# An attention and FFN kernel: pooled sums of v and the mask on TensorE, g applied at w_out's rounding, and a new order of the steps

## The chip, the cores and the metric

The kernel runs on one core of one Trainium2 chip. The metric is the device time of one execution in microseconds (us). A core has five engines that run side by side, each through its own list of instructions in a fixed order: PE (TensorE, matrix products; PEld is its weight load), DVE (VectorE), ACT (ScalarE), POOL (GpSimd) and SP (SyncE), which issues the transfers (DMAs). SBUF is the on-chip memory, PSUM the memory into which PE writes.

## The reference

For each of 8 batches and 8 heads (576 positions, 64 channels) two attentions are added: one over q, k and v averaged over groups of 4 positions, its result repeated 4 times, and one over the band of positions nearer than 4. The sum, as 4608 rows of 512, goes through an FFN with a SoLU and a layer norm.

```python
q_d, k_d, v_d = (t.reshape(B, H, S // 4, 4, D).mean(axis=3) for t in (q, k, v))
out_up = np.repeat(sm_attn(q_d, k_d, v_d), 4, axis=2)
mask = np.abs(pos[:, None] - pos[None, :]) < 4
scores = np.where(mask, scale * (q @ k.T), -1e9)
attn_out = out_up + softmax(scores) @ v
h = x @ w_in                                  # x: 4608 x 512, w_in: 512 x 1024
solu = h * softmax(h)
ln = (solu - mean) / np.sqrt(var + 1e-6) * g_ln
out = ln @ w_out                              # w_out: 1024 x 512
```

The weights come in as float64; the kernel takes their two 32-bit words apart itself.

## The kernel before

**Start.** `Weights.piece` turns 16 pieces of the weights (512 KB each; 0 to 7 are w_in, 8 to 15 w_out) into two parts, `hi` (`wi_h`, `wo_h`) and `lo` (`wi_l`, `wo_l`), of 128x512. A piece takes one pass of ACT (`L323`), four of DVE (`L325`, `L329`, `L334`, `L338`), for w_out a pass of ACT that multiplies by g (`L358`), then ACT's rounding to `hi` (`L360`) and POOL's subtraction that leaves `lo` (`L362`). `keep_clock` is 24 times two products of zeros that nobody reads (`L947`, tile `warm`), placed among the steps of PE.

**Attention of a batch.** `EarlyBatch` (batches 0 and 1) turns q and k on PE (`qp`, `kp`, `L478`) and copies them on ACT (`L484`); later batches turn them on DVE (`L411`, `L415`). Sums over 4 positions (`L367`) give `qd` and `kd`. The pooled v, `vd`, comes from v loaded a second time (`vs`, `L275`) and added up on POOL in two steps (`L434`, `L437`). `Local` does the band: ten windows of 64 positions, two at a time (u = 0 to 4). PE makes the scores (`sc`, `L614`), DVE adds the mask (`L632`) and takes the maximum (`L637`), POOL subtracts it (`L639`), ACT takes the exponential (`L641`), DVE sums and inverts (`L644`, `L648`), POOL multiplies (`L650`), PE turns the result (`plt`, `L660`), ACT copies it (`plT`, `L663`), PE multiplies by the window's v (`vw`; `xp`, `L670`), and the result is added to x (`L496`, `L498`). `Pooled` does the same for the averages, a pair of heads at a time (`sd` `L696`, `mxd` `L703`, `pd` `L711` to `L720`, `pdt` `L731`, `pdT` `L738` to `L743`, `po` `L752`).

**FFN.** Tile i holds 128 of the 4608 rows. `xhl` splits x into `xh` and `xl` (`L919`, `L922`); `ffn_in` is 24 products of 128x512 into `h` (`L770`), a maximum on DVE (`nmx`, `L778`), the exponential on ACT (`L782`), and `e` on DVE (`L785`), which frees h's only buffer. u goes out to memory and back (`L813`, `L845`), DVE turns it in blocks (`L866`), ACT and POOL split it (`uh` `L872`, `ul` `L874`), and `ffn_out` is 24 products into `o` (`L888`).

**What sets the order.** All steps are numbered in a plan of 2099; `ORDER` is a table that lists every number once, and the instructions are recorded in that sequence. Each engine runs its own in that order. Semaphores are added where one engine needs another's result.

Of the kernel before, what the change touches and what calls it, by code (L numbers as in the profile page):

```python
# [129 lines left out]
def pooled_local_attention_then_solu_ffn(  # L130
# [10 lines left out]
    nc = tc.nc  # L141
# [27 lines left out]

    EARLY = 2  # L170
    MASKED = 0
    W_PSUM = False
    WARM = 24

    def rows(n):
# [866 lines left out]
```

## Time and profile before

| | before |
|---|---|
| time, median of 3 runs | 602.74 us (602.57 to 603.37) |
| the profiled execution's own time | 602.74 us |
| its span, first to last instruction | 601.0 us |
| PE busy | 574.8 us, 96% |
| DVE, POOL, ACT busy | 396.5, 375.6, 361.8 us |
| granted PE clock, mean | 0.989 |

The time of a run is 1.74 us longer than the span of the same execution. Busy time is the union of an engine's instructions; two that follow each other overlap by some hundredths of a us in the records, so a sum of mean durations is a few per cent over the busy time.

### The profile page before, as it was taken

The page shows a single profiled execution, that of the slowest core. Times are in us where ns is not written, and L with a number is a line of the kernel's source. Part 1 is how long each engine was busy: PE and PEld are TensorE (multiplying, and loading weights), DVE is VectorE, ACT ScalarE, POOL GpSimd, SP SyncE. Part 2 cuts the span into 40 slices and gives each one's busy share as a digit, 9 for nine tenths or more (in the row PEclk, how much of TensorE's full clock was granted, in tenths as well). Part 3 has the DMA queues.
Part 4 walks back from the last instruction along what each step waited for, and adds up shares of the span by engine and source line. Part 5 has one row for each costly group of instructions (what it writes and reads, how often), then busy time and mean ns, then how long its engine had stood idle before and what let it go on. Part 6 is the DMA issues. An engine that isn't in the chain of part 4 may idle for free.

```text
span 601.0 us, 15341 instructions
## 1 busy us (share of the span) xinstructions
PE 574.8 (96%) x5912; PEld 447.1 (74%) x5912; DVE 396.5 (66%) x692; ACT 361.8 (60%) x800; POOL 375.6 (62%) x553
## 2 busy tenths in 40 slices
PE   6889789899999999999999999999999999999996
PEld 3666557677777777787877777777777878788785
DVE  5989999869747677766856767737655533643541
ACT  3758866577745566566664854657465655553443
POOL 2576668867784778678574777656786767332221
PEclk8979999899999999999999999999999999999999
DMA  8999776687769767766878567847416623124230
GB/s 231 238 251 254 140 183 146 164 178 162 195 144 189 171 167 186 170 148 175 190 151 201 143 173 182 185 114 195 97 59 188 146 89 114 63 88 151 96 123 35
DMA packets 203913, 94.34 MB, mean 157 GB/s; under 512 B 162496, under 2 KB 192704, under 8 KB 203840
## 3 DMA queue, kind: packets, MB, share of 16 engines
q1 hardware_dynamic: 203840, 93.37, 63.3%
q8 instruction: 46, 0.75, 0.6%
q14 instruction: 27, 0.22, 0.1%
HBM read 65.54 MB, written 27.79 MB: 155 GB/s over the span
## 4 chain that ended last, share of the span: by engine, by line
PE 75%; POOL 6%; DVE 5%; ACT 4%; SPq 4%; DMA 3%; issue 3%; POOLq 0%; DVEq 0%
PE o L888 31%; PE h L770 27%; PE xp L670 3%; PE plt L660 3%; PE po L752 3%; PE sc L614 2%; DMA qm<-in_q_dram 2%; SPq L245 2%; PE pdt L731 2%; PE sd L696 2%; POOL pl L639 2%; DMA v<-u 1%; SPq L264 1%; POOL pd L720 1%; DVE w L334 1%
## 5 line engine op out<-in xcount | busy, mean ns | idle before, releaser
L888 PE MATMUL o<-wo_h,uh 128*128 128x512 f32 x288 | 117.9, 409 | 0.8 <-ACT uh L872 0.7
L770 PE MATMUL h<-wi_h,xh 128*128 128x512 f32 x288 | 116.3, 404 | 0.6 <-DVE e L785 0.6
L770 PE MATMUL h<-wi_h,xl 128*128 128x512 f32 x288 | 114.3, 397 | 1.3 <-POOL xl L922 1.3
L888 PE MATMUL o<-wo_l,uh 128*128 128x512 f32 x288 | 114.5, 398 | 0.0
L770 PE MATMUL h<-wi_l,xh 128*128 128x512 f32 x288 | 114.1, 396 | 0.0
L874 POOL TENSOR_TENSOR ul<-v,uh 128x512 fp32r<-128x512 f32 x58 | 74.4, 1288 | 19.7 <-ACT uh L872 7.7
L778 DVE TENSOR_REDUCE nmx<-h 128x1 f32<-128x1024 f32 x36 | 43.9, 1219 | 63.8 <-PE h L770 63.8
L888 PE MATMUL o<-wo_h,ul 128*128 128x512 f32 x288 | 79.1, 396 | 0.4 <-DVE ul L874 0.4
L782 ACT ACTIVATE e<-h,nmx 128x1024 f32<-128x1024 f32 x36 | 40.0, 1112 | 51.0 <-DVE nmx L778 51.0
L888 PEld LDWEIGHTS o<-wo_h,uh 128*128 128x128 f32 x288 | 54.6, 190 | 15.6 <-ACT uh L872 1.4
L770 PEld LDWEIGHTS h<-wi_h,xl 128*128 128x128 f32 x288 | 54.2, 188 | 15.2 <-POOL xl L922 2.1
L770 PEld LDWEIGHTS h<-wi_h,xh 128*128 128x128 f32 x288 | 54.2, 188 | 14.8 <-issue 1.0
L888 PEld LDWEIGHTS o<-wo_h,ul 128*128 128x128 f32 x288 | 54.2, 188 | 14.0 <-DVE ul L874 0.8
L770 PEld LDWEIGHTS h<-wi_l,xh 128*128 128x128 f32 x288 | 54.3, 189 | 12.2
L888 PEld LDWEIGHTS o<-wo_l,uh 128*128 128x128 f32 x288 | 54.5, 189 | 11.8
L922 POOL TENSOR_TENSOR xl<-x,xh 128x512 fp32r<-128x512 f32 (+1 forms) x40 | 47.1, 1183 | 18.6 <-ACT xh L919 17.4
L807 ACT ACTIVATE e<-e,nmu 128x1024 f32<-128x1024 f32 x35 | 40.1, 1146 | 28.2 <-POOL nmu L790 28.1
L785 DVE SCALAR_TENSOR_TENSOR e<-h,e 128x1024 f32<-128x1024 f32 x36 | 43.7, 1214 | 19.9 <-ACT e L782 19.9
L650 POOL TENSOR_TENSOR pl<-pl,rsl 128x512 f32<-128x512 f32 x40 | 42.1, 1055 | 20.7 <-DVE rsl L648 18.2
L866 DVE STREAM_TRANSPOSE v<-v 128x512 f32<-128x512 f32 x70 | 46.3, 688 | 12.5 <-DMA v<-u 12.5
L872 ACT ACTIVATE uh<-v 128x512 fp32r<-128x512 f32 x70 | 42.9, 623 | 14.9 <-DVE v L866 11.0
L639 POOL TENSOR_TENSOR pl<-pl,mxl 128x512 f32<-128x512 f32 x40 | 41.8, 1052 | 9.0 <-DVE mxl L637 4.6
(95 smaller groups left out, 1076.1 us busy)
## 6 DMA issues: line engine op xcount, KB each, us to landing
u<-e SPq DMA_DIRECT2D x35, 512.0 KB
v<-u SPq DMA_DIRECT2D x140, 128.0 KB
vw<-in_v_dram SPq DMA_DIRECT2D x160, 64.0 KB
vs<-in_v_dram SPq DMA_DIRECT2D x32, 288.0 KB
out_dram<-osb SPq DMA_DIRECT2D x36, 256.0 KB
qm<-in_q_dram SPq DMA_DIRECT2D x96, 72.0 KB
km<-in_k_dram SPq DMA_DIRECT2D x96, 72.0 KB
w<-in_moe_w_out_dram SPq DMA_DIRECT2D x8, 512.0 KB
```

What stands on the lines that cost most here:

```text
L639: nc.gpsimd.tensor_tensor(out=pl, in0=pl, in1=max_bc, op=ALU.subtract)
L650: nc.gpsimd.tensor_tensor(out=pl, in0=pl, in1=rs.unsqueeze(3).broadcast_to([P, NPR, 2, W]), op=ALU.mult)
L770: nc.tensor.matmul(hps[:, n, :], src[:, cc, :], wt[:, cc, n * 512:(n + 1) * 512], start=(cc == 0 and src is xh and wt is wi_h), stop=(cc = ...
L778: nc.vector.tensor_reduce(out=nmx, in_=hf, op=ALU.max, axis=AX.X, negate=True)
L782: nc.scalar.activation(e, hf, AF.Exp, bias=nmx, scale=1.0, accum_out=se)
L785: nc.vector.scalar_tensor_tensor(out=e, in0=hf, scalar=1.0, in1=e, op0=ALU.mult, op1=ALU.mult, accum_out=su)
L807: nc.scalar.activation(e, e, AF.Identity, bias=nmu, scale=1.0)
L866: nc.vector.transpose(vg, vg)
L872: nc.scalar.activation(uh, tp, AF.Copy)
L874: (nc.vector if v is None or i in LATE else nc.gpsimd).tensor_tensor(out=ul, in0=tp, in1=uh.bitcast(F32), op=ALU.subtract)
L888: nc.tensor.matmul(o, src[:, j, :], wt[:, 4 * g + j, :], start=(g == 0 and j == 0 and src is uh and wt is wo_h), stop=(g == 1 and j == 3 a ...
L922: nc.gpsimd.tensor_tensor(out=l, in0=src, in1=h.bitcast(F32), op=ALU.subtract)
```

## The change

1. **Pooled sums of batch 0 on PE** (`SUMS_ON_PE = 1`). `vd` of batch 0 is no longer added up on POOL from a second load of v. `pool_steps` multiplies the local part's tiles `vw` by band matrices of zeros and ones: 20 products, two chunks (`vp`) of five windows and two halves; ACT copies one half of a chunk, DVE adds the other. `make_bands` builds the bands once (a memset on POOL, three sums on DVE). Batch 0 so needs all five `vw` ahead of its pooled part, and its four loads of `vs` (288 KB each) are gone.
2. **Mask by PE in batches 0 and 1** (`MASKED = 2`). Two products of 128x256 in bf16 (`ident_b` by `mask_b`) put the mask into the scores' bank, and the scores are added to it. DVE takes the maximum from PSUM and subtracts it itself, so POOL's subtraction and one step of the plan go, ten times in all. `keep_clock` multiplies `ident_b` in place of zeros.
3. **g at the rounding** (`G_LATE`). For w_out, g is the scale of ACT's rounding pass, and DVE forms `lo` as w times g minus `hi` in one instruction (`scalar_tensor_tensor`); the pass of ACT over w and POOL's subtraction go, eight times.
4. **Other engines** (`OTHER`). 145 steps in a second table run on another engine than usual: among them, new on DVE, are 11 `e<-e,nmu`, 25 `ul`, 17 `xl`, 11 each of `pl` minus maximum and `pl` times `rsl`, 9 `pd`, 6 pairs of the pooled sums, 10 `plT` and 8 copies to x; the first DVE pass of 9 weight pieces (`L325`) goes to POOL.
5. **A new order**: `ORDER` is another table (2088 steps now).

```diff
 ORDER = """
-181 0 182 1 2 3 165 25 183 166 4 5 6 184 167 185 24 26 186 187 188 27 7 8 173 32 168 169 170
...
+159 11 16 3 2 160 161 162 9 56 19 24 167 168 169 170 26 171 172 173 25 163 27 33 32 164 174 165
...
+OTHER = """
+29 84 95 104 161 174 185 209 217 225 257 265 273 281 355 498 518 519 523 565 567 573 592 598
...
-    MASKED = 0
-    W_PSUM = False
+    MASKED = 2
     WARM = 24
+    SUMS_ON_PE = 1
+    G_LATE = True
...
+    if MASKED:
+        filler = ident_b
...
+    GR = SD // 2
+    BAND = {0: (0, 16), 1: (3, 15), 3: (1, 15)}
+    bands = {}
+
+    def make_bands():
+        t = moe.tile([P, DFF], F32, tag="e", name="bands")[:, 0:3 * 160]
+        t = t.rearrange("p (r x) -> p r x", r=3)
+        nc.gpsimd.memset(t, 0.0)
+        by_half = ident.rearrange("p (h k) -> p h k", h=2)
+        for n, (r, (off, m)) in enumerate(BAND.items()):
+            nc.vector.tensor_reduce(
+                out=t[:, n, GR:GR + m],
+                in_=by_half[:, :, off:off + FAC * m].rearrange("p h (j i) -> p j h i", i=FAC),
+                op=ALU.add, axis=AX.XY,
+            )
+            bands[r] = t[:, n]
...
+    other = {int(n) for n in OTHER.split()}
+    now = [None]
+
+    def engine(usual, instead):
+        return instead if now[0] in other else usual
...
-            nc.vector.tensor_scalar(
+            engine(nc.vector, nc.gpsimd).tensor_scalar(
                 out=t, in0=t, scalar1=F64_LO, scalar2=F64_HI, op0=ALU.max, op1=ALU.min
             )
...
-                nc.scalar.activation(t, t, AF.Copy, scale=self.g[:, fc:fc + 1])
+                g = self.g[:, fc:fc + 1]
                 hi, lo = wo_h[:, fc, :], wo_l[:, fc, :]
+                if G_LATE:
+                    nc.scalar.activation(hi, t, AF.Copy, scale=g)
+                    yield
+                    nc.vector.scalar_tensor_tensor(
+                        out=lo, in0=t, scalar=g, in1=hi.bitcast(F32), op0=ALU.mult, op1=ALU.subtract
+                    )
+                    yield
+                    return
...
+        def pool_steps(self):
+            firsts = [-(-s0 // FAC) for s0 in starts]
+            ends = firsts[1:] + [SD]
+            for c in range(2):
+                tp = two_banks(ps_h, "h", f"vp_{self.b}_{c}")[0:GR]
+                at = tp.rearrange("p h (r a d) -> p h r a d", r=NPR, a=2)
+                ws = range(5 * c, 5 * c + 5)
+                for w in ws:
+                    s0, g0, g1 = starts[w], firsts[w], ends[w]
+                    at0 = GR - (g0 - GR * c)
+                    K = FAC * g1 - s0
+                    for half in range(2):
+                        nc.tensor.matmul(
+                            at[:, half, :, half ^ (w % 2), :],
+                            bands[s0 % FAC][half * W:half * W + K, at0:at0 + GR],
+                            self.vw[w // 2][half * W:half * W + K, w % 2],
+                            start=w == ws[0], stop=w == ws[-1],
+                        )
+                yield
+                vd = self.vd[:, c].rearrange("p h d -> p (h d)")
+                nc.scalar.activation(vd, tp[:, 0], AF.Copy)
+                yield
+                nc.vector.tensor_tensor(out=vd, in0=vd, in1=tp[:, 1], op=ALU.add)
+                yield
...
     def attention(bt):
-        values(bt)
+        by_pe = bt.b < SUMS_ON_PE
+        late = bt.b == 0
...
+        if by_pe:
+            if not bt.b:
+                step(make_bands)
+            for u in range(5):
+                step(bt.load_v, u)
+            row(bt.pool_steps(), 6)
+        else:
+            values(bt)
...
     for n in ORDER.split():
-        fn, args = plan[int(n)]
+        now[0] = int(n)
+        fn, args = plan[now[0]]
         fn(*args)
```

In the rows below a name is a tile with its indices and a buffer's number. Three places show the new order. The first is DVE's list where the last two pieces of w_out, 14 and 15, are made ready. Before:

```order
L644 TENSOR_REDUCE sml_4_1493<-pl_106 128x8
L648 RECIPROCAL rsl_4_1495<-sml_4_1493 128x8
L325 TENSOR_SCALAR w_14_1480<-w_14_1480 128x512
L325 TENSOR_SCALAR w_15_1497<-w_15_1497 128x512
L329 TENSOR_SCALAR w_15_1497<-w_15_1497 128x512
L329 TENSOR_SCALAR w_14_1480<-w_14_1480 128x512
L334 SCALAR_TENSOR_TENSOR w_15_1497<-w_15_1220,w_15_1497 128x512
L334 SCALAR_TENSOR_TENSOR w_14_1480<-w_14_1064,w_14_1480 128x512
L338 SCALAR_TENSOR_TENSOR w_15_1497<-w_15_1220,w_15_1497 128x512
L338 SCALAR_TENSOR_TENSOR w_14_1480<-w_14_1064,w_14_1480 128x512
```

Here piece 14 leaves DVE with its last row, and ACT and POOL do the rest. The same place of DVE's list after:

```order
L374 TENSOR_SCALAR w_15_1628<-w_15_1628 128x512
L423 TENSOR_REDUCE kd_1638<-kT_1472 128x144
L379 SCALAR_TENSOR_TENSOR w_15_1628<-w_15_1232,w_15_1628 128x512
L379 SCALAR_TENSOR_TENSOR w_14_1563<-w_14_1437,w_14_1563 128x512
L383 SCALAR_TENSOR_TENSOR w_15_1628<-w_15_1232,w_15_1628 128x512
L907 RECIPROCAL r_1660<-se_1374 128x1
L467 STREAM_TRANSPOSE kT_1472<-km_998 128x576
L471 STREAM_TRANSPOSE qT_1695<-qm_997 128x576
L383 SCALAR_TENSOR_TENSOR w_14_1563<-w_14_1437,w_14_1563 128x512
L423 TENSOR_REDUCE kd_1638<-kT_1472 128x144
L408 SCALAR_TENSOR_TENSOR wo_l<-w_15_1628,g_sb,wo_h 128x512
L408 SCALAR_TENSOR_TENSOR wo_l<-w_14_1563,g_sb,wo_h 128x512
```

The first pass of each piece is gone from the list (it is POOL's), steps of batch 2 stand in between, and the subtraction that makes `wo_l` ends the sequence on DVE. The second place is PE's list early in batch 0, around the third pair of windows. Before:

```order
L614 MATMUL sc_1_416<-kT_158,qT_157 64x64 x16
L731 MATMUL pdt_0_444<-ident,pd_0_269 72x64 x12
L614 MATMUL sc_2_463<-kT_158,qT_157 64x64 x16
L614 MATMUL sc_3_501<-kT_158,qT_157 64x64 x16
L478 MATMUL qp_2_527<-ident,qm_458 64x96 x12
L752 MATMUL po_0_542<-pdT_0_457,vd_304 64x144 x4
```

After:

```order
L691 LDWEIGHTS ident_b
L691 MATMUL sc_2_464<-mask_b,ident_b 128x256
L698 MATMUL sc_2_464<-kT_166,qT_165 64x64 x16
L510 MATMUL vp_0_488<-vw_0_346,bands 72x4x64 x4
L510 MATMUL vp_0_488<-vw_1_267,bands 72x4x64 x4
L510 MATMUL vp_0_488<-vw_2_424,bands 72x4x64 x2
```

The mask's products stand ahead of the scores, and the first chunk of the pooled sums has moved onto PE behind them. The third place is POOL's list in batch 0. Before:

```order
L362 TENSOR_TENSOR wi_l<-w_4_250,wi_h 128x4x4x32
L434 TENSOR_TENSOR vs_1_0_413<-vs_1_0_413 72x4x128
L437 TENSOR_TENSOR vd_304<-vs_1_0_413 72x256
L639 TENSOR_TENSOR pl_105<-pl_105,mxl_0_411 128x4x128
L720 TENSOR_TENSOR pd_2_434<-pd_2_434,rsd_2_440 128x432
L639 TENSOR_TENSOR pl_106<-pl_106,mxl_1_442 128x4x128
L650 TENSOR_TENSOR pl_105<-pl_105,rsl_0_495 128x4x128
```

After:

```order
L416 TENSOR_TENSOR wi_l<-w_4_358,wi_h 128x4x4x32
L806 TENSOR_TENSOR pd_2_432<-pd_2_432,rsd_2_519 128x432
L736 TENSOR_TENSOR pl_107<-pl_107,rsl_0_603 128x4x128
L370 TENSOR_SCALAR w_7_563<-w_7_563 128x512
L736 TENSOR_TENSOR pl_108<-pl_108,rsl_1_685 128x4x128
```

The pooled sums and the subtractions of the maximum are gone from it, and a first pass over a weight piece stands there.

More of the change, by code (lines that the diff above doesn't have):

```diff
@@ L26 @@
 ORDER = """
[99 rows of a table removed]
[99 rows of a table added]
+"""
+OTHER = """
[8 rows of a table added]
 """
@@ L233, in small_bank @@
     def small_bank(b, n):
-        return (ps_o, "o") if b < 2 and n % 2 and not W_PSUM and not WARM else (ps_t, "t")
+        return (ps_o, "o") if b < 2 and n % 2 and not WARM else (ps_t, "t")
     def load_q_k(t, b, pr):
@@ L320, in f32 @@
             w = moe.tile([P, DO], F32, tag="osb", name=f"w32_{n}", bufs=2)
-            t = ps_o.tile([P, DO], F32, tag="o", name=f"wb_{n}") if W_PSUM else w
+            t = w
             ti = t.bitcast(I32)
@@ L495, in accumulate @@
         if first:
-            nc.scalar.activation(x, part, AF.Copy)
+            copy(engine(nc.scalar, nc.vector), x, part)
         else:
@@ L616, in by_tensor @@
                         bt.qT[rows(par), pr, s0:s0 + W], bt.kT[rows(par), pr, s0:s0 + W],
-                        start=not early, stop=True,
+                        start=not early, stop=not early or pr == NPR - 1,
                     )
@@ L638, in by_tensor @@
                 yield
-                nc.gpsimd.tensor_tensor(out=pl, in0=pl, in1=max_bc, op=ALU.subtract)
+                engine(nc.gpsimd, nc.vector).tensor_tensor(
+                    out=pl, in0=pl, in1=max_bc, op=ALU.subtract
+                )
                 yield
@@ L662, in by_tensor @@
             plT = wk.tile([P, NPR, 2, W], F32, tag="plT", name=f"plT_{b}_{u}")
-            nc.scalar.activation(plT, pt, AF.Copy)
+            copy(engine(nc.scalar, nc.vector), plT, pt)
             yield
@@ L737, in steps @@
             yield
-            nc.scalar.activation(pdT[:, :, :, 0, :], pt[:, 0], AF.Copy)
+            copy(engine(nc.scalar, nc.vector), pdT[:, :, :, 0, :], pt[:, 0])
             yield
-            if b < 2:
-                nc.scalar.activation(pdT[:, :, :, 1, :], pt[:, 1], AF.Copy)
-            else:
-                nc.vector.tensor_copy(out=pdT[:, :, :, 1, :], in_=pt[:, 1])
+            copy(
+                engine(nc.scalar, nc.vector) if b < 2 else engine(nc.vector, nc.scalar),
+                pdT[:, :, :, 1, :], pt[:, 1],
+            )
             yield
@@ L806, in ffn_in @@
         else:
-            nc.scalar.activation(e, e, AF.Identity, bias=nmu, scale=1.0)
+            if engine(nc.scalar, nc.vector) is nc.scalar:
+                nc.scalar.activation(e, e, AF.Identity, bias=nmu, scale=1.0)
+            else:
+                nc.vector.tensor_scalar(
+                    out=e, in0=e, scalar1=1.0, scalar2=nmu, op0=ALU.mult, op1=ALU.add
+                )
         s = small.tile([P, 1], F32, tag="s", name=f"s_{i}", bufs=6)
@@ L940, in pooled_local_attention_then_solu_ffn @@
     weights = Weights()
-    idle = []
     def keep_clock(n):
-        if not idle:
-            idle.append(ps_o.tile([P, 512], F32, tag="o", name="warm"))
+        o = ps_o.tile([P, 512], F32, tag="o", name=f"warm_{n}")
         for _ in range(2):
             nc.tensor.matmul(
-                idle[0].rearrange("p (a n) -> p a n", n=P), zeros,
-                zeros.unsqueeze(1).broadcast_to([P, 4, P]), start=True, stop=True,
+                o.rearrange("p (a n) -> p a n", n=P), filler,
+                filler.unsqueeze(1).broadcast_to([P, 4, P]), start=True, stop=True,
             )
@@ L981, in attention @@
     def attention(bt):
-        values(bt)
-        local = [Local(bt, u, bt.b > 0) for u in range(5)]
-        pooled = [Pooled(bt, pr, bt.b == 0) for pr in range(NPR)]
-        for it in pooled + local if bt.b == 0 else local + pooled:
-            if isinstance(it, Local):
+        by_pe = bt.b < SUMS_ON_PE
+        late = bt.b == 0
+        local = [Local(bt, u, not late) for u in range(5)]
+        pooled = [Pooled(bt, pr, late) for pr in range(NPR)]
+        if by_pe:
[4 more added lines that the diff above has]
+            row(bt.pool_steps(), 6)
+        else:
+            values(bt)
+        for it in pooled + local if late else local + pooled:
+            if isinstance(it, Local) and not by_pe:
                 step(bt.load_v, it.u)
```

37 lines of the change are left out of this document (24 added, 13 removed), and 203 rows, old and new, of tables (ORDER, OTHER).

## The prediction

> **What bounds the kernel now.** I read the page first (busy shares), then the sums by stage, then the order of time around the end of the start-up stage, then the groups by line.
>
> ```profile
> span 601.0 us, 15341 instructions
> PE 574.8 (96%) x5912; PEld 447.1 (74%) x5912; DVE 396.5 (66%) x692; ACT 361.8 (60%) x800; POOL 375.6 (62%) x553
> ```
>
> PE is busy for 96% of the span, so over the whole kernel only less work on PE, or fewer gaps in it, can shorten the time. Where the gaps are, the busy times by stretch say (stretch, its length, then PE, PEld, DVE, ACT, POOL, the granted PE clock, DMA share, GB/s):
>
> ```profile
> 0.00:15.00 15.00, 9.96 (x58) 4.92 (x60) 8.22 (x17) 4.95 (x7) 3.44 (x13) 0.89 0.89 231
> 15.00:63.00 48.00, 41.02 (x811) 31.52 (x805) 43.98 (x77) 36.25 (x99) 30.29 (x29) 0.93 1.00 239
> 63.00:106.20 43.20, 37.84 (x462) 28.57 (x462) 42.27 (x70) 30.34 (x64) 31.54 (x34) 1.00 0.74 162
> 106.20:118.00 11.80, 9.34 (x218) 7.47 (x218) 9.91 (x17) 7.38 (x14) 10.36 (x13) 0.86 0.61 160
> 118.00:188.20 70.20, 70.08 (x700) 54.77 (x701) 50.46 (x91) 44.20 (x99) 50.27 (x76) 1.00 0.77 173
> 188.20:400.00 211.80, 211.46 (x2208) 166.51 (x2209) 143.45 (x252) 130.66 (x299) 146.38 (x211) 1.00 0.73 171
> ```
>
> From 118 us on PE has no gap worth the name (0.12 us to 188.2, 0.34 to 400). Up to 118 us it idles 5.04 + 6.98 + 5.36 + 2.46 = 19.8 us, and what is saturated there is DVE: 43.98 of 48.0, then 42.27 of 43.2. So the start-up is DVE's, and its length decides when PE's unbroken work begins. How the stage ends:
>
> ```profile
> 105.00 1.28 DVE L338 SCALAR_TENSOR_TENSOR w<-w,w 128x512 int32<-128x512 int32 x2
> 105.72 0.72 ACT L358 ACTIVATE w<-w,g_sb 128x512 f32<-128x512 f32 x1 [2.09 <-DVE w L338]
> 109.30 0.88 PE L660 MATMUL plt<-ident,pl 128*128 128x128 f32 x4 [2.46 <-ACT plT L663]
> 111.17 0.80 PE L888 MATMUL o<-wo_h,uh 128*128 128x512 f32 x1
> 113.25 0.40 PE L888 MATMUL o<-wo_l,uh 128*128 128x512 f32 x1
> ```
>
> DVE gives the last pieces of w_out at 106.28 (start and length of the first row), ACT stands 2.09 us waiting for them and has four passes (L358 and L360 of two pieces) queued ahead of the copy that PE needs, PE waits 2.46 us, and at 111.17 the second half of the first output tile starts. It is the last piece of PE work with a wait of that size ahead of it.
>
> **The change, part by part.** The sum is made at one point of PE's work: the product of that second half that first needs `wo_l` of piece 14, its sixth (four for pieces 12 and 13 ahead of it, then `wo_h` of 14); the useful work of PE behind that point is the same before and after. Before, it started at 113.25 (last row). In the new order DVE makes `wo_l` itself, so the point follows from when DVE is through its list up to there. These are the groups that carry the sum (busy us, mean ns of one):
>
> ```profile
> L325 DVE TENSOR_SCALAR w<-w 128x512 f32<-128x512 f32 x16 | 12.9, 814 | 5.6 <-ACT w L323 5.6
> L329 DVE TENSOR_SCALAR w<-w 128x512 int32<-128x512 int32 x16 | 9.2, 587 | 0.2
> L338 DVE SCALAR_TENSOR_TENSOR w<-w,w 128x512 int32<-128x512 int32 x12 | 8.0, 683 | 0.1
> L874 DVE TENSOR_TENSOR ul<-v,uh 128x512 fp32r<-128x512 f32 x12 | 9.0, 765 | 7.6 <-ACT uh L872 5.5 <-issue 2.1
> L632 DVE TENSOR_TENSOR pl<-sc,mask 128x512 f32<-128x512 f32 x40 | 26.7, 675 | 12.8 <-PE sc L614 12.7
> L743 DVE COPY pdT<-pdt 72x288 f32<-72x288 f32 x24 | 10.6, 444 | 14.5 <-ACT pdT L738 14.5
> L411 DVE STREAM_TRANSPOSE kT<-km 128x576 f32<-128x576 f32 x24 | 18.1, 759 | 0.0
> L367 DVE TENSOR_REDUCE kd<-kT 128x144 f32<-128x576 f32 x32 | 23.4, 738 | 0.8 <-ACT kT L484 0.6
> L648 DVE RECIPROCAL rsl<-sml 128x8 f32<-128x8 f32 x40 | 8.1, 203 | 1.9
> ```
>
> *DVE, added up to `wo_l` of 14.* Eight `wo_l`: the nearest row is `ul` (same output, two inputs in SBUF), 8 x 0.765 = 6.1. Four `pdT`, 1.8. One kT copy and the two additions to `vd` from PSUM, as L632, 2.0. One `wi_l`, 0.8. The bands: no row shows them; between L648 and L367, 3 x 0.2 to 0.7; they read few elements, so 0.25 each, 0.8; two casts at 0.2, 0.4. Work of batch 2 that now stands ahead (two transposes, one `kd`, one reciprocal), 2.4. Sum 14.3.
>
> *DVE, taken away.* Nine first passes over weight pieces, 9 x 0.814 = 7.3. The mask changes nothing here: L632 and the maximum become a maximum and a subtraction, two passes over 512 each.
>
> Net 7.0; in the records neighbours overlap (two of 0.683 took 1.28 above), so some 6.4. Before, DVE had 8.22 + 43.98 + 42.27 = 94.5 us of work to 106.2; after, 100.9.
>
> *POOL.* It loses, in the start-up, work of these rows, and gets nine passes that no row shows on POOL (between 0.7, as the smaller L437, and 1.4, as L362; I take 1.05, as L639):
>
> ```profile
> L362 POOL TENSOR_TENSOR wi_l<-w,wi_h 128x512 fp32r<-128x512 f32 x8 | 11.0, 1375 | 24.1 <-ACT wi_h L360 24.1
> L362 POOL TENSOR_TENSOR wo_l<-w,wo_h 128x512 fp32r<-128x512 f32 x8 | 10.4, 1299 | 11.2 <-ACT wo_h L360 11.1
> L434 POOL TENSOR_TENSOR vs<-vs 72x512 f32<-72x512 f32 x32 | 41.4, 1293 | 0.6
> L437 POOL TENSOR_TENSOR vd<-vs 72x256 f32<-72x256 f32 x32 | 23.8, 742 | 2.5
> L639 POOL TENSOR_TENSOR pl<-pl,mxl 128x512 f32<-128x512 f32 x40 | 41.8, 1052 | 9.0 <-DVE mxl L637 4.6
> ```
>
> Lost: 10 x 1.05 + 4 x (1.29 + 0.74) + 1.4 + 8 x 1.30 = 30.4; got: 9.5; so 21 of the 30.29 + 31.54 + 3.4 us it had to 106.2. POOL is no bound there; but its work delays DVE's:
>
> ```profile
> 11.09 1.37 POOL L362 TENSOR_TENSOR wi_l<-w,wi_h 128x512 fp32r<-128x512 f32 x1 [8.57 <-ACT wi_h L360]
> 11.37 1.64 DVE L338 SCALAR_TENSOR_TENSOR w<-stage,w 128x512 int32<-128x512 int32 x1
> 21.71 0.41 DVE L325 TENSOR_SCALAR w<-w 128x512 f32<-128x512 f32 x1
> 537.18 1.29 POOL L922 TENSOR_TENSOR xl<-x,xh 128x512 fp32r<-128x512 f32 x1
> 537.99 1.63 DVE L874 TENSOR_TENSOR ul<-v,uh 128x512 fp32r<-128x512 f32 x2 [0.23 <-ACT uh L872]
> ```
>
> Alone a pass of L325 takes 0.41 us (third row), on the mean 0.814. L338 at 11.37 ends at 13.01, 0.55 after POOL's end, 0.96 over the mean of 0.683. The `ul` pair of 537.99 ends at 539.62, 1.15 after POOL's end, and two free ones take 1.28 as the L338 pair does: they ran when POOL was through, some 0.3 over. So of the passes that stay, 7 x 0.40 (L325), 16 x 0.18 (L329 against 0.41) and that 0.96 are waits: 6.6. With a third less work on POOL (21 of 65) a third of it goes, 2.2 us; the ends are nothing and all 6.6. That gives 100.9 - 2.2 = 98.7 us.
>
> The Trainium skill (SBUF — State Buffer, "Who interferes with whom") states this as a rule: a DVE instruction with two SBUF inputs, and GpSimd instructions that read SBUF, shut each other out for a whole instruction. The trace agrees (the 537.99 row). By the rule, what moves from POOL to DVE keeps the wait and only changes the engine that pays for it; what it would do to the time is the second rival.
>
> *DVE's idle time.* Before: 6.78 us in the first 15 us, 4.02 to 63, 0.93 to 106.2. The first stays: it is the arrival of the first pieces. Of the second a known piece is this:
>
> ```profile
> 38.43 0.61 DVE L703 TENSOR_REDUCE mxd<-sd 128x3 f32<-128x432 f32 x1 [1.54 <-PE sd L696]
> ```
>
> That `sd` stood on PE behind `po`, whose `vd` came from POOL, the queue that loses the sums and subtractions. I take 1.0 of the 4.02 as gained; the ends are 4.02 gained and 3 us lost, the latter if the hops over POOL that the nine passes add (ACT, POOL, DVE) stand in the way. So 10.7 us idle, and DVE is through at 98.7 + 10.7 = 109.4. The point that was at 113.25 comes 3.8 us earlier.
>
> *PE, added.* Twenty products for the mask and twenty for the sums.
>
> ```profile
> 57.81 0.60 PE L947 MATMUL warm<-zeros 128*128 128x512 bf16 x2
> 51.85 0.71 PE L752 MATMUL po<-pdT,vd 72*64 72x144 f32 x8
> ```
>
> A mask product has half the columns of a warm one: 20 x 0.15 = 3.0. Four products of `po` (eight records) take 0.71; at 256 columns in place of 144 that is 0.32 each, 6.3 for twenty, 3.2 if halves run side by side and 12.6 if they stand apart as `po`'s do not. In all 6 to 16, I take 9. All stand in the stretch where PE idles 19.8 us and does 24 x 0.60 = 14 us of `warm` (24 pairs, the first row's length for each), which stay, some at other places. DVE sets the pace there, so 9 us cost nothing as long as PE's own work to the point, which then leaves some 11 us of idle, is not the longer one. At 16 us it leaves 4, and part of it would show.
>
> *ACT* loses eight passes of L358 and gets two copies of `vp`; *SP* loses four `vs` loads (1.2 MB) and brings five `vw` forward; the DMA share is 1.00 to 63 us, but DVE's waits there are on PE and ACT, so this is worth nothing to the sum.
>
> *Behind the point.* Up to the ninth tile's maximum (188.2 before) DVE had 9.91 + 50.46 = 60.4 us of work; by the build it now has some 15 two-input steps of POOL more there, and copies, 74 in all, in 79 us. PE then waits where a DVE step comes late; the first places are the scores of batch 2 and the second output tile. I take 1.6 of the 3.8 us as given back. From 188.2 DVE's load goes from 68% (143.45 of 211.8) to some 80%, which I cost at nothing: a step that is late by a POOL instruction has other tiles' products of PE in between.
>
> **Sum.** 601.0 - 3.8 + 1.6 = 598.8 us span; the execution shown was itself the median run, 1.74 us above its span: 600.5 us.
>
> **The rivals.**
>
> *No difference.* DVE is through at 100.9 + 11.7 = 112.6 (no relief, idle as before): the gain at the point is 0.6 us, and as much of new waits takes it. For it: DVE's list is longer, not shorter. Time 602.7.
>
> *Slower: the port.* In the 79 us behind the point DVE is full. Each of its 15 new two-input steps can find POOL at work: 0.3 us in the 537.99 pair, and up to the 1.29 of POOL's `xl` if that has just begun. At 0.5 us each it is 7.5 us, DVE then needs 81 of 79, and batch 2's scores and tiles 4 to 8 come late on PE. If the point also comes at 112.6 and half of the 7.5 reaches PE: 602.7 - 0.6 + 3.8 = 606. It decides once the new waits pass the slack of about 5 us. Against it: DVE kept 98% busy from 63 to 106 with the same neighbour.
>
> *Much faster.* All idle of 15 to 63 us but 1 us goes (3.0), and most of POOL's delays (another 2.5): 600.5 - 2.0 - 2.5 = 596. For it: POOL loses a third of its work, ACT eight passes of L358 (8 x 0.72 = 6 us).
>
> **How the numbers follow.** Forecast (598 to 601.5) 0.37, much faster 0.15, no difference 0.20, slower 0.28. What a measurement here can tell from no change is 0.2%, 601.5 to 604. The range goes from 594.5, below the much faster case, to 608, above the slower one. Faster 0.52, same 0.20, slower 0.28.
>
> **What would show it.** Right: the last `wo_l` on DVE near 109, DVE over 95% busy from 15 to 185 us, PE without gaps from some 115, `vp` and the mask's products with PE idle around them. Wrong: PE gaps between 115 and 190 that end on DVE; `ul`, `xl` or `pl` on DVE with means above 0.9 us; PE idle to 118 below 8 us, so that PE's added work shows; or a first weight piece that is ready later.

## The result: 1.0% slower, and the profile after

| | before | after |
|---|---|---|
| time, median (range, runs) | 603.06 us (602.57 to 604.32, 4) | 608.89 us (608.08 to 610.96, 4) |
| ratio to before, 95% interval | | 1.0099 (1.0074 to 1.0124) |
| profiled execution: time, span | 602.74, 601.0 us | 608.08, 605.9 us |

Executions of one kernel differ by up to 1.7%, and a trace shows one of them.

The page of the changed kernel, its head (busy time, share of the span, instructions):

```profile
span 605.9 us, 15391 instructions
PE 580.7 (96%) x5972; PEld 446.9 (74%) x5972; DVE 478.9 (79%) x814; ACT 337.4 (56%) x764; POOL 290.1 (48%) x450
```

PE has 5.9 us more of busy time, POOL 85 us less, DVE 82 us more. The busy times by stretch, for the same stretches as in the prediction (PE, PEld, DVE, ACT, POOL, granted PE clock, DMA share, GB/s):

```profile
0.00:15.00 15.00, 11.10 (x112) 5.70 (x112) 9.42 (x23) 4.63 (x7) 5.23 (x13) 1.00 0.88 260
15.00:63.00 48.00, 42.26 (x769) 30.39 (x766) 42.64 (x77) 33.52 (x94) 25.46 (x20) 1.00 0.87 219
63.00:106.20 43.20, 37.84 (x490) 27.20 (x489) 42.23 (x71) 28.82 (x61) 26.96 (x25) 0.96 0.71 160
106.20:118.00 11.80, 10.55 (x165) 7.84 (x167) 11.80 (x19) 5.44 (x9) 6.01 (x12) 1.00 0.54 140
118.00:188.20 70.20, 69.36 (x778) 54.64 (x774) 66.06 (x113) 41.31 (x94) 42.73 (x65) 1.00 0.80 179
188.20:400.00 211.80, 208.69 (x2182) 162.74 (x2181) 176.41 (x298) 121.28 (x284) 108.41 (x171) 1.00 0.66 159
```

Up to 118 us PE idles 3.90 + 5.74 + 5.36 + 1.25 = 16.3 us (19.8 before), so most of its new work went into idle time; DVE has no idle left between 106.2 and 118 us. From 118 to 400 us PE idles 0.84 + 3.11 us where it idled 0.12 + 0.34. The granted clock of PE is not what made the kernel slower: behind 118 us it is 1.00 in both, and ahead of it 1.00, 1.00, 0.96 and 1.00 in these stretches, where before it was 0.89, 0.93, 1.00 and 0.86. The end of the start-up, on DVE and on PE (timeline: start, length):

```profile
110.96 1.43 DVE L383 SCALAR_TENSOR_TENSOR w<-w,w 128x512 int32<-128x512 int32 x1
112.31 0.74 DVE L423 TENSOR_REDUCE kd<-kT 128x144 f32<-128x576 f32 x1
112.97 1.40 DVE L408 SCALAR_TENSOR_TENSOR wo_l<-w,g_sb,wo_h 128x512 fp32r<-128x512 f32 x2
113.19 0.49 PE L980 MATMUL o<-wo_h,uh 128*128 128x512 f32 x1 [0.52 <-ACT wo_h L406]
114.42 0.50 PE L980 MATMUL o<-wo_l,uh 128*128 128x512 f32 x1 [0.74 <-DVE wo_l L408]
```

The last two `wo_l` end at 114.37, and the product that the prediction counted to (the first with `wo_l` of piece 14) starts at 114.42, released by them. Before, it started at 113.25. PE's instructions ahead of it and behind it are the same in number in both traces, but for the 60 records of the new products, all ahead. So the 4.9 us of span split exactly: 1.2 us ahead of the point, and 605.9 - 114.4 = 491.5 in place of 601.0 - 113.25 = 487.75 behind it, 3.7 us. Forecast were -3.8 and +1.6. Of the 3.7 us behind the point, 2.5 are idle time of PE (8.9 in place of 6.4); the other 1.2 are longer busy time of the same products, for which no run gives a cause. What PE waited for behind the point, up to 560 us (us in total, times, longest; the five largest of changed, then the two of before):

```profile
PE h L856 <- DVE e L871: 1.2, 2, 0.8
PE o L980 <- ACT osb L987: 0.9, 2, 0.7
PE o L980 <- ACT uh L963: 0.8, 1, 0.8
PE po L838 <- DVE x L582: 0.4, 1, 0.4
PE xp L756 <- DVE pdT L269: 0.3, 1, 0.3
PE sc L614 <- issue: 0.9, 1, 0.9
PE pdt L731 <- ACT pd L711: 0.3, 1, 0.3
```

### The profile page after: what moved, and what is told of

The parts are those of the page before. It is cut to its first block, busy times and chain, and to the rows that moved or that the text cites. A ratio compares the mean times of both kernels' runs of the same rounds, so it can differ in the third digit from the quotient of the medians.

```text
span 605.9 us, 15391 instructions
## 1 busy us (share of the span) xinstructions
PE 580.7 (96%) x5972; PEld 446.9 (74%) x5972; DVE 478.9 (79%) x814; ACT 337.4 (56%) x764; POOL 290.1 (48%) x450
## 4 chain that ended last, share of the span: by engine, by line
PE 65%; DVE 14%; DMA 8%; SPq 4%; issue 4%; ACT 3%; POOL 1%; DVEq 0%; POOLq 0%; ACTq 0%
PE o L980 27%; PE h L856 24%; PE xp L756 3%; PE sc L698 2%; PE plt L746 2%; PE po L838 2%; DMA w<-in_moe_w_in_dram 2%; PE sd L782 2%; PE pdt L817 1%; SPq L309 1%; SPq L290 1%; DMA vs<-in_v_dram 1%; DVE sml L730 1%; DMA u<-e 1%; DVE nmx L864 1%
## 5 line engine op out<-in xcount | busy, mean ns | idle before, releaser
L966 POOL TENSOR_TENSOR ul<-v,uh 128x512 fp32r<-128x512 f32 x33 | 43.4, 1317 | 52.1 <-ACT uh L963 40.4
L856 PEld LDWEIGHTS h<-wi_l,xh 128*128 128x128 f32 x288 | 54.3, 189 | 11.9
L987 ACT ACTIVATE osb<-o,s 128x512 f32<-128x512 f32 x36 | 24.5, 682 | 40.5 <-PE o L980 12.2
L736 POOL TENSOR_TENSOR pl<-pl,rsl 128x512 f32<-128x512 f32 x29 | 31.2, 1079 | 27.9 <-DVE rsl L734 27.9
L1014 POOL TENSOR_TENSOR xl<-x,xh 128x512 fp32r<-128x512 f32 x23 | 30.2, 1315 | 25.7 <-ACT xh L1011 25.4
L966 DVE TENSOR_TENSOR ul<-v,uh 128x512 fp32r<-128x512 f32 x37 | 29.0, 794 | 12.0 <-ACT uh L963 11.9
```

The source lines that it names most:

```text
L736: engine(nc.gpsimd, nc.vector).tensor_tensor(out=pl, in0=pl, in1=rs.unsqueeze(3).broadcast_to([P, NPR, 2, W]), op=ALU.mult)
L856: nc.tensor.matmul(hps[:, n, :], src[:, cc, :], wt[:, cc, n * 512:(n + 1) * 512], start=(cc == 0 and src is xh and wt is wi_h), stop=(cc = ...
L966: (usual if v is None else engine(usual, nc.vector)).tensor_tensor(out=ul, in0=tp, in1=uh.bitcast(F32), op=ALU.subtract)
L987: nc.scalar.activation(osb, o, AF.Copy, scale=s)
L1014: engine(nc.gpsimd, nc.vector).tensor_tensor(out=l, in0=src, in1=h.bitcast(F32), op=ALU.subtract)
```

## The experiments

All were timed in five rounds against the kernel before (whose median was 602.2 to 603.0 us in these groups). For each, the point is where the first product with `wo_l` of 14 starts in its trace, and the rest is the span of that execution less the point. Both belong to the one execution whose time the third column gives.

| kernel | time, us | traced, us | ratio to before (95%) | point | rest |
|---|---|---|---|---|---|
| before | 603.06 | 602.74 |  | 113.25 | 487.75 |
| changed | 608.89 | 608.08 | 1.0099 (1.0074 to 1.0124) | 114.42 | 491.5 |
| e1 passes back on DVE | 608.06 | 607.37 | 1.0078 (1.0053 to 1.0103) | 113.64 | 491.7 |
| e2 moves behind undone | 626.20 | 625.15 | 1.0374 (1.0343 to 1.0406) | 113.87 | 509.5 |
| e3 no moves | 626.07 | 622.77 | 1.0372 (1.0340 to 1.0405) | 111.62 | 509.4 |
| e4 products twice | 612.81 | 612.84 | 1.0157 (1.0125 to 1.0190) | 118.49 | 492.1 |
| e5 products left out | 607.98 | 611.32 | 1.0083 (1.0052 to 1.0114) | 116.17 | 492.9 |
| e6 g late for two pieces | 614.85 | 614.88 | 1.0192 (1.0167 to 1.0217) | 121.36 | 491.7 |
| e7 sums back on POOL | 611.68 | 607.96 | 1.0161 (1.0123 to 1.0199) | 114.27 | 491.9 |
| e9 one pass left out | 603.95 | 601.45 | 1.0022 (1.0000 to 1.0044) | 108.59 | 490.6 |
| h1 new start, old tail | 609.96 | 611.27 | 1.0118 (1.0090 to 1.0147) | 115.47 | 493.9 |
| h2 old start, new tail | 611.61 | 613.97 | 1.0148 (1.0118 to 1.0177) | 114.79 | 497.4 |
| b1 before, g late | 608.62 | 610.02 | 1.0104 (1.0073 to 1.0134) | 120.63 | 487.6 |
| b2 before, g late for two | 605.23 | 603.51 | 1.0042 (1.0019 to 1.0064) | 113.45 | 488.3 |
| b3 before, masked | 598.18 | 598.35 | 0.9924 (0.9894 to 0.9954) | 109.86 | 486.7 |
| b4 before, sums | 609.51 | 610.10 | 1.0103 (1.0066 to 1.0140) | 120.96 | 487.3 |
| b6 before, masked, g late | 605.22 | 607.22 | 1.0051 (1.0024 to 1.0078) | 117.80 | 487.2 |
| b12 masked, POOL kept early | 617.85 | 621.34 | 1.0263 (1.0220 to 1.0306) | 132.18 | 487.4 |
| b13 masked, POOL kept in place | 604.74 | 606.38 | 1.0038 (1.0010 to 1.0066) | 117.04 | 487.6 |
| b15 before, masked, sums | 607.57 | 604.44 | 1.0081 (1.0050 to 1.0112) | 116.28 | 485.9 |

The last column is the first finding. Leave the two joined kernels (h) and the two without moves (e2, e3) aside: every kernel with the tail of before has a rest of 485.9 to 488.3, every one with the changed tail 490.6 to 492.9, though their points differ by up to 22 and 13 us. So the 3.7 us behind the point go with the tail. In all of these the tail follows a variant of its own start-up; what h1 and h2, which cross the two, add to that stands below.

One part of the change is not named among its five and has no run of its own: each pair of products of `keep_clock` now writes a tile of its own, where before all 24 wrote the same one. The kernels e and h1 do it the new way, b and h2 the old one. In the traces of before and changed only the first of these products waits, for its input (to 2.3 and 3.3 us).

### What sets the changed start-up

e1: the nine first passes go back to DVE.

```diff
-29 84 95 104 161 174 185 209 217 225 257 265 273 281 355 ...
+29 84 95 104 174 355 ...
```

> The changed kernel with one thing undone: the nine first passes over weight pieces (L370) go from POOL back to DVE. Theory A (the end of DVE's list sets the start-up, and POOL's passes of 1.97 us hold DVE's next passes up: L374 at 0.711, L379 at 0.876, L383 at 0.796 us where free ones take 0.43 and 0.69, together 8 us): DVE gets 9 x 0.41 to 0.81 = 3.7 to 7.3 us of work and loses most of the 8 us of waits and the hops over POOL; time 605 to 607. Theory B (PE's added products, some 7 us, set the time): no change, 608.4 to 609.4. Theory C (the steps moved to DVE behind the start-up make PE wait): no change either.

608.06 us, as much as the changed kernel within the intervals, and not the 605 to 607 of theory A; the point 0.8 us earlier. Nine passes more on DVE cost nothing, or: taking them off had gained nothing. Up to the point DVE is busy 104.3 us and idle 9.3, in place of 102.5 and 11.9.

e4 and e5: the new products issued twice, and for the most part left out.

```diff
-                for a in range(2):
+                for a, last in ((0, True), (1, True), (0, False), (1, False)):      # e4; the sums: for _ in range(2)
-                ws = range(5 * c, 5 * c + 5)
+                ws = range(5 * c, 5 * c + 2)                                        # e5; the mask's products are gone
```

> The changed kernel with each of the 40 new products on PE (20 for the mask, 20 for the sums) issued twice, same result. They are 10.4 us of busy time in the records, some 7 us in which PE takes nothing else. Theory A (DVE sets the start-up, PE has 16 us of idle there): at most 1.5 us more, 608.5 to 610.5. Theory B (PE's added work sets the time): 615 to 617.

> The changed kernel without the 20 mask products and without 12 of the 20 products of the sums (the softmax of two batches is then not masked and the pooled sums take two of five windows); everything else, the order and DVE's steps, as changed. Issued twice, the 40 products cost 3.9 us in the first group of runs. Theory A (DVE's list sets the start-up; the second copy only overfilled PE): 608 to 609, less than 1 us gained. Theory B (PE's products stand in the chain of the start-up: DVE waits for scores and sums that come behind them): 604 to 606.

Twice: 3.9 us more, between the two theories. Left out: 0.9 us less, inside the intervals (the traced execution took 611.32 us, so its late point says nothing). The products once are covered by PE's idle time; a second copy no longer is (in that trace DVE is busy 38.3 of the 48 us from 15 to 63 us, in place of 42.6: it then waits for PE).

e9: DVE's last pass over the eight pieces of w_out is left out.

```diff
-            nc.vector.scalar_tensor_tensor(out=w.bitcast(I32), in0=lo, scalar=29, in1=ti, ...
+            if n < 8:
+                nc.vector.scalar_tensor_tensor(out=w.bitcast(I32), in0=lo, scalar=29, in1=ti, ...
```

> The changed kernel without DVE's last pass (L383) over the eight pieces of w_out, so that the lowest three bits of these weights stay zero: 8 x 0.69 = 5.5 us less in DVE's list ahead of the point. Theory A (DVE's list sets the end of the changed start-up): 603 to 605.5. Rival (loads, PE or ACT stand right behind, or the tail takes the gain back): 607 to 609.

```profile
108.59 0.40 PE L981 MATMUL o<-wo_l,uh 128*128 128x512 f32 x1
```

5.5 us off DVE's list: the point 5.8 us earlier, the time 4.9 us less. DVE's list sets the end of the changed start-up: shown.

e6: the g at the rounding, and so `wo_l` by DVE, for pieces 14 and 15 alone.

```diff
-                if G_LATE:
+                if n >= 14:
```

> The changed kernel with w_out's g at the rounding (and so wo_l by DVE) for pieces 14 and 15 alone; pieces 8 to 13 go the way of before: ACT multiplies and rounds, POOL subtracts. DVE's list loses 6 x 0.74 = 4.4 us, ACT gets 6 x 0.72, POOL 6 x 1.3 = 7.8. Theory A (DVE's list sets the end of the start-up): 604.5 to 607. Rival: POOL's subtractions come late or hold DVE up by as much: 608 to 612.

6 us more in place of 2 to 4 less. The order was made for DVE's `wo_l`; POOL's subtractions now stand at those places of its queue, wait there for ACT, and the split of x is behind them (waits of PE):

```profile
PE h L856 <- POOL xl L1014: 4.7, 1, 4.7
```

e7: the sums back on POOL in the new order, with their four loads (`SUMS_ON_PE = 0`, the steps put at the places of those that went).

> The changed kernel with the first batch's sums back on POOL: four loads of 288 KB and four times 1.3 + 0.8 us of POOL in the places where the new order loads v and makes the products; the loads of v as far ahead of their use as before. DVE's list loses three reductions and two additions, 1.9 us, and gets POOL's neighbours back. Theory A (DVE's list): 606 to 609. Rival (the sums' loads or POOL's instructions cost more than the products, so the change gains by this part): 610 to 614.

611.68 us, 0.5% over the changed kernel; but the intervals touch, and the points agree within 0.2 us. That the sums' products gain in the new order is not shown, and not excluded.

### Which part costs what in the order of before

```diff
+                if True:            # b1;  b2: if n >= 14
+                    nc.scalar.activation(hi, t, AF.Copy, scale=g)
+                    yield
+                    nc.vector.scalar_tensor_tensor(out=lo, in0=t, scalar=g, in1=hi.bitcast(F32), op0=ALU.mult, op1=ALU.subtract)
```

> The kernel before with one part of the change alone: w_out's g at the rounding, wo_l of all eight pieces by DVE; its own order. DVE's list gets 8 x 0.74 = 5.9 us; the lag from DVE's last weight pass (106.28) to the first product with wo_l of 14 (113.25), 7.0 us over ACT and POOL, shrinks to some 1.5. Theory A: 602 to 604, no difference. Rival (ACT's and POOL's relief is worth something in the start-up): 598 to 601.

> The kernel before with w_out's g at the rounding for pieces 14 and 15 alone. DVE's list gets 1.5 us, the lag of 7.0 us at its end shrinks to some 1.5. Theory A: 598 to 600. Rival (other pieces' subtractions on POOL, or PE's other work, are as late): 601.5 to 603.5.

b1 loses 1.0%, its point comes 7.4 us later. DVE's list is longer by eight passes, 7.8 us with their waits, and the passes that stood last in it were held up more (the first row is two of L325 that take 0.41 alone; the same two took 1.81 before):

```profile
105.71 4.15 DVE L325 TENSOR_SCALAR w<-w 128x512 f32<-128x512 f32 x2
120.63 0.63 PE L897 MATMUL o<-wo_l,uh 128*128 128x512 f32 x1
```

b2 gains nothing at the point (113.45): what it takes off one place it loses at another. DVE's last pass ends at 108.29 in place of 106.28, because two of L329 take 4.53 us there in place of 2.18; the way from it to the product takes 5.2 us in place of 7.0. In both kernels that way goes over ACT's copy `plT`, which stands behind ACT's passes over the last two pieces, and from there on PE works without a gap up to the product:

```profile
109.98 0.63 PE L669 MATMUL plt<-ident,pl 128*128 128x128 f32 x4 [4.03 <-ACT plT L672]
113.45 0.63 PE L897 MATMUL o<-wo_l,uh 128*128 128x512 f32 x1
```

So the two subtractions on POOL that b2 takes away were not what the product waited for; before, they end at 109.72.

b3: the mask of two batches alone (`MASKED = 2`; the maximum and the subtraction from PSUM both at the place of the mask's addition, POOL's ten subtractions gone). b13 and b12 give POOL ten subtractions of zeros back: b13 at the place where the old ones stood, b12 at the place of DVE's new subtraction.

```diff
                 nc.vector.tensor_tensor(out=pl, in0=sc, in1=max_bc, op=ALU.subtract)
                 yield
+                yield                                                                        # b13
+                nc.gpsimd.tensor_tensor(out=pl, in0=pl, in1=zero8..., op=ALU.subtract)      # b13; b12: ahead of the yields
+                yield
```

> The kernel before with the mask of two batches by TensorE alone, in its own order: DVE's passes are as many (a maximum and a subtraction from PSUM, put at the place of the mask's addition), POOL loses ten subtractions L639, behind four of which DVE waited 3.4 us in the start-up; PE gets 3 to 4 us of products. Theory A (DVE's waits go with the POOL instruction): 599 to 601.5. Rival (DVE waits behind the next instruction of POOL in its place, as after the passes were moved): 602 to 604.

> The kernel before with the mask by TensorE (598.2), and in the place of each of the ten subtractions L639 that POOL lost, a subtraction of zeros by POOL of the same shape, in the same chain ahead of the exponential. Theory A (the gain is POOL's instruction: DVE's waits behind it and the hop over POOL): 601 to 603. Rival (the gain is DVE's two passes from PSUM or the new clock of PE): 598 to 599.5.

> As the kernel with the mask alone (598.2), but with POOL's subtraction of zeros at the very place in the order at which the subtraction L639 stood before, ten times; DVE's maximum and subtraction from PSUM stay. So against the kernel before, the instructions of POOL are the same and only DVE's two passes and PE's products differ. Theory A (the gain is POOL's instruction that goes): 601.5 to 604. Rival (the gain lies in the other passes): 598 to 600.

```profile
109.86 0.40 PE L972 MATMUL o<-wo_l,uh 128*128 128x512 f32 x1
117.04 0.39 PE L979 MATMUL o<-wo_l,uh 128*128 128x512 f32 x1
PE h L853 <- POOL xl L1011: 7.4, 2, 3.9
```

b3 (first row) is 0.76% faster than before: the point comes 3.4 us earlier. With POOL's ten instructions in place (second row) the gain is gone and more: the point is 7.2 us later than b3's. So the mask gains because POOL's instruction goes. Not by DVE's waits behind it, though: the first passes over the weights take the same mean in both (the second ones 0.53 and 0.62):

```profile
L362 DVE TENSOR_SCALAR w<-w 128x512 f32<-128x512 f32 x16 | 10.8, 687 | 4.6 <-ACT w L360 4.6
L365 DVE TENSOR_SCALAR w<-w 128x512 f32<-128x512 f32 x16 | 10.8, 687 | 5.6 <-ACT w L363 5.6
```

What differs more is DVE's idle time: up to the point it is busy 98.8 us and idle 11.1 in b3, busy 100.9 and idle 16.1 in b13. Some 2 us of that are not POOL's doing: the first maximum from PSUM starts at 29.3 in b3 and at 31.3 in b13, ahead of POOL's first subtraction. That the rest is the hop over POOL in the chain of a softmax, and the place that it takes in POOL's queue, is argued. b12 shows that the place matters: the same ten instructions some steps earlier in the queue (third row) hold the split of x up, and cost 13 us more.

b4 and b15: the sums by band products in the order of before, in two placements; b15 with the mask too.

> The kernel before with the first batch's sums by band products alone: the five loads of v, which before stood later, take the places of the four loads for the sums (1.2 MB less in the first 60 us, where the DMA share is 1.00); POOL loses 4 x 2.03 us; DVE gets three reductions and two additions, 1.9 us by the changed kernel's trace; PE some 6 us. Theory A (DVE's list sets the start-up): 602.5 to 605. Rival (the loads are what the start-up waits for): 598.5 to 601.

> The kernel before with the mask and the sums by TensorE, its order, loads of v spread as in the changed kernel (each behind q and k of the pair that is needed first), products at the 117th and 128th step. Theory A (the sums lost in the order of before by their place alone; in the new order they gain 2.8 us, and the mask gains 4.0): 595 to 598. Rival (the sums lose wherever they stand in this order): 601 to 606.

b4 is 1.0% slower than before, b15 1.6% slower than b3. In b15, DVE's waits to 120 us:

```profile
DVE vd L512 <- ACT vd L510: 7.6, 2, 4.5
```

The addition of the two halves stands in DVE's queue and waits for ACT's copy of the products, 7.6 us in which the full engine does nothing. In the changed order the same two waits are 1.4 us. The place counts for much; that there is a place in the order of before where the sums gain was not found in two tries.

b6: mask and g together.

> The kernel before, in its order, with the mask by TensorE and w_out's g at the rounding (wo_l by DVE). Alone the mask gained 4.0 us and the g lost 5.8. Theory A (DVE's list: the two add up): 602.5 to 605.5. Rival (the g lost only because POOL's subtractions L639 held the full DVE up, and these are gone here): 598 to 601.

605.22 us: above the sum of the two (598.2 + 5.8 = 604.0) by no more than the intervals allow. The g at the rounding loses 7.9 us at the point here too.

### The tail

e2 and e3: the moves behind the point undone, then all of them (`OTHER` cut to the 15 steps that stand ahead of the point, then empty).

> The changed kernel with only the 15 engine moves kept that stand ahead of wo_l of piece 14 in the order; the 130 behind it go back to their usual engines (POOL, ACT), in the same order. Theory C (of the 4.3 us in which PE waits behind the point, 3.1 more than before, the cause is DVE, which is 84% busy between 300 and 400 us): time 605 to 606.5. Theory A and B: these waits come from the order, not from the engines; with POOL's slower steps back they grow; 609 to 613.

> The changed kernel with all 145 engine moves undone, in the same order: products for the mask and the sums, w_out's g at the rounding, and the order alone remain. Theories A and C together: 602 to 605. Theory B: 608 to 609.

Both 626 us, above every time expected, the rest 509: behind the point the changed order without its moves is 18 us worse, in the main because POOL comes late (the longest wait of PE in e2):

```profile
PE plt L739 <- POOL pl L729: 9.2, 3, 4.8
```

So what the moves cost against before cannot be read from undoing them here. e3's point, 111.62, is the earliest of the whole start-up as changed, 2.8 us ahead of the changed kernel's (traced at 622.77 us): that the moves ahead of the point gain anything there is not shown.

h1 and h2: the two kernels joined behind the first output tile (the steps done by there are not quite the same ones in the two).

```diff
+ORDER = changed[:522] + [steps left, in the order of before]      # h1, 18 moves
+ORDER = before[:562] + [steps left, in the changed order]         # h2, 126 moves
```

> The changed kernel up to and with the first output tile (522 of its 2088 steps, 18 engine moves among them); behind it the order and the engines of before. By the two traces the start-up lost 1.2 us (the point came at 114.42 in place of 113.25) and what lies behind it 3.7 us, with the same products of PE. Theory A (two separate losses that add up): 603.5 to 605. Rival (the new start-up hands DVE's backlog on, so the tail is late whatever its order): 606 to 609.

> The kernel before up to just behind its first output tile (562 of 2099 steps); behind it the order and the engine moves of the change. No products for mask or sums, w_out as before. Theory A (two separate losses): 605.5 to 607. Rival (the tail's waits come from the new start-up): 602 to 604.

Both are slower than either theory said, h2 more than any: between 118 and 188 us PE idles 3.3 and 3.9 us, and its granted clock is 0.95 there in place of 1.00, so the joint itself costs time. Behind that the rows can be compared (118 to 188.2, then 188.2 to 560 us; h1, h2, and for the second stretch before and changed):

```profile
118.00:188.20 70.20, 66.87 (x766) 52.30 (x767) 50.87 (x89) 40.57 (x91) 49.32 (x70) 0.95 0.64 154
188.20:560.00 371.80, 370.24 (x3525) 290.94 (x3524) 229.18 (x407) 222.48 (x497) 242.01 (x368) 1.00 0.58 148
118.00:188.20 70.20, 66.30 (x668) 51.47 (x665) 55.90 (x94) 38.98 (x91) 39.62 (x60) 0.95 0.78 172
188.20:560.00 371.80, 368.53 (x3575) 288.33 (x3574) 288.83 (x494) 205.51 (x473) 176.66 (x291) 1.00 0.57 145
188.20:560.00 371.80, 370.45 (x3524) 291.25 (x3524) 227.24 (x400) 221.97 (x494) 243.35 (x368) 1.00 0.59 147
188.20:560.00 371.80, 368.12 (x3501) 288.14 (x3500) 287.84 (x489) 206.58 (x471) 175.82 (x292) 1.00 0.55 144
```

PE idles 1.6 us there with the old tail behind the new start, 3.3 with the new tail behind the old start; before 1.4, changed 3.7. So with either start-up the new tail idles more in this stretch, by 1.7 us (h2 against h1) and 2.3 (changed against before), with DVE at 77 or 78% in place of 61 or 62%: that much of the 3.7 us is the tail's own.

## Why the prediction was wrong, point by point

**Right: what bounds the start-up.** DVE's list did, after (e9) and by all signs before (b1). PE's new products were covered (e5), and PE idled 16.3 us to 118 in place of the 11 that were reckoned with.

**Wrong: where DVE is through.** Forecast were 98.7 us of work and 10.7 idle, 109.4. Measured, to 114.37: DVE busy 102.45 us, idle 11.9.

```profile
0.00:114.37 114.37, 98.16 (x1453) 68.41 (x1453) 102.45 (x180) 69.64 (x166) 61.17 (x62) 0.99 0.80 199
```

The list itself was near: less its waits it is 93.1 us, where 100.9 - 6.6 = 94.3 were reckoned with. The step that failed is the relief: "With a third less work on POOL (21 of 65) a third of it goes, 2.2 us". The groups say how (x, busy us, mean ns):

```profile
L374 DVE TENSOR_SCALAR w<-w 128x512 int32<-128x512 int32 x16 | 11.4, 711 | 6.2 <-POOL w L370 6.0
L379 DVE SCALAR_TENSOR_TENSOR w<-w,w 128x512 int32<-128x512 int32 x12 | 10.4, 876 | 0.1
L383 DVE SCALAR_TENSOR_TENSOR w<-w,w 128x512 int32<-128x512 int32 x12 | 9.5, 796 | 0.2
L370 DVE TENSOR_SCALAR w<-w 128x512 f32<-128x512 f32 x7 | 4.1, 587 | 0.3 <-ACT w L368 0.3
L370 POOL TENSOR_SCALAR w<-w 128x512 f32<-128x512 f32 x9 | 17.8, 1973 | 10.7 <-ACT w L368 10.6
```

Against 0.43 (L374), 0.69 (L379, L383) and 0.42 (L370) alone, the passes waited 16 x 0.28 + 12 x 0.19 + 12 x 0.11 + 7 x 0.17 = 9.3 us; before, by the same reckoning, 16 x 0.40 + 16 x 0.16 + 8 x 0.24 = 10.9. Nine of the sixteen passes that waited most had left, and the next passes waited in their place: 9.3 us where 6.6 - 2.2 = 4.4 were forecast, 4.9 of the 5.0 us by which DVE was through later (1.2 us more idle time than forecast were made good by the shorter list). The 6.6 were too few as well: a second pass of 1.65 us (one of L334 at 15.02) was left out, and by the reckoning here the passes that stayed had waited 10.9 - 9 x 0.40 = 7.3 us. So their waits rose by 2.0 us where they were to fall by 2.2. e1 says the same from the other side: with the nine passes back on DVE, the four groups wait 6.9 us.

**Wrong: the price of POOL's passes.** 1.97 us, not 1.05, outside the bounds of 0.7 to 1.4. So POOL's work to 106.2 us fell from 65.3 to 57.7 us, by 8 and not 21, and DVE stood idle 6.0 us for these passes (first row), 4.4 of it at the first piece (before, it stood 5.6 us for ACT's pass ahead of them). The gain of 1.0 us of idle time did not come: 11.9 us up to the point, 11.7 before up to 106.2.

**Too small: what is given back.** 1.6 us were forecast behind the point, 3.7 came. DVE was as full as forecast between 118 and 188 (66.1 of 70.2), yet PE lost only 0.84 us there. The step that failed is DVE's load from 188.2 on, "which I cost at nothing": it went to 83% by 400, and PE idled 2.3 us more than before between 188 and 560.

**The rivals.** The slower case gave 606, nearest to the 608.9. Of its two conditions, no relief at the point and waits of the moved steps, the first held and went further; the second came, but mostly behind 188 us. Its price of 0.5 us for a wait was too high, as the 37 `ul` on DVE show (0.794 us, where 0.69 is the mean of the two that read PSUM), so what it called the port is not shown to be the tail's cause:

```profile
L966 DVE TENSOR_TENSOR ul<-v,uh 128x512 fp32r<-128x512 f32 x37 | 29.0, 794 | 12.0 <-ACT uh L963 11.9
L966 DVE TENSOR_TENSOR ul<-ut,uh 128x512 fp32r<-128x512 f32 x2 | 1.4, 692 | 3.4 <-ACT uh L963 3.4
```

DVE's greater share of busy time stands beside the waits there; that it makes them was argued, not tried alone.

**Not seen at all.** The parts are worth very different things. The mask, put at nothing for DVE, gains 0.76% alone, and loses the gain when POOL's instructions come back (b13). The g at the rounding costs 7 to 8 us at the point in the order of before. What g and the sums would be worth in an order fitted to each stays open: every kernel that undoes or adds one part at a fixed order also measures how badly that order then fits (e2, e3, e6, b4).

The version that beats both is b3: the kernel before with the mask of two batches by TensorE, 598.18 us, 0.9924 of before.

## What to carry to other kernels

Where a full engine waits behind a neighbour, moving the instruction that waits need not take the wait away: here the next ones in the queue inherited it. Look instead for an instruction of the neighbour that can go altogether, as the mask's subtraction did. A change that comes with a new order should be taken apart in the old one first, part by part, and the split of the time at one product with equal work on both sides tells which half of the program paid.

## What the runs showed of the hardware

POOL's passes with one input (`L370`) did not hold DVE up; instructions with two did. In the changed kernel (POOL, then DVE):

```profile
79.15 2.07 POOL L370 TENSOR_SCALAR w<-w 128x512 f32<-128x512 f32 x1 [0.25 <-ACT w L368]
80.04 0.67 DVE L383 SCALAR_TENSOR_TENSOR w<-w,w 128x512 int32<-128x512 int32 x1
101.61 1.05 POOL L736 TENSOR_TENSOR pl<-pl,rsl 128x512 f32<-128x512 f32 x1
101.68 1.26 DVE L374 TENSOR_SCALAR w<-w 128x512 int32<-128x512 int32 x1
102.63 2.09 POOL L370 TENSOR_SCALAR w<-w 128x512 f32<-128x512 f32 x1
```

L383, with two inputs in SBUF, took its 0.67 us in the middle of POOL's pass; L379 at 89.46 and L408 at 100.27 did the same (0.68 and 0.74 us). L374 waited for the end of POOL's multiplication (102.66) and was done 0.28 us later, while POOL's next pass with one input ran (last row). Of the 14 passes over weights that took DVE over 0.1 us too long in this trace, 13 overlap an instruction of POOL with two inputs, and the first, at 7.78, a memset. The 13 end behind that instruction by the same time in each: the TENSOR_SCALARs 0.28 to 0.29 us behind its end, the SCALAR_TENSOR_TENSORs 0.55. The Trainium skill (SBUF — State Buffer, "Who interferes with whom") has a DVE instruction with two SBUF inputs contend with a GpSimd instruction that reads SBUF; the second row does not agree with that, the fourth agrees with what it says of TENSOR_SCALAR. A pass over 128x512 with a maximum and a minimum takes POOL 1.97 us where DVE takes 0.42 alone.
